# The first chunk of a windowed-attention and gated-FFN layer: layer norm tile by tile, its roots on GpSimd, and a first weight block for both halves of the array

## The chip, the cores and the metric

One NeuronCore of a Trainium2 chip runs one program. The metric is the device time of that program in microseconds, median of several runs. The engines are named as the profile names them: PE (TensorE), with PEld for its weight loads, DVE (VectorE), ACT (ScalarE), POOL (GpSimd) and SP (SyncE, which issues nearly all DMAs here). A "q" behind a name (SPq) is that engine's instruction queue. A column is one fp32 element of a partition.

## The reference

```python
def reference(A_x, A_wqkv, A_wo, B_x, B_w_gate, B_w_up, B_w_down):
    x = A_x                                   # (1, 2048, 512)
    xn = _layernorm(x, axis=-1)               # (x - mean) / sqrt(var + 1e-5)
    s = _A_ref(xn, A_wqkv, A_wo)              # 32 heads of 16, causal window of 256, softmax, @ wo
    g = _silu(_B_ref(xn, B_w_gate, B_w_up, B_w_down))   # (silu(xn@w_gate) * (xn@w_up)) @ w_down
    return x + s * g
```

The widths are D = 512 and F = 1792; everything is fp32. `B_x` is not used.

## The kernel before, in words

The 2048 tokens are worked on in four chunks of 512 (`c` = 0 to 3). For a chunk, `load_x(c)` fetches four tiles `xt` of 128 tokens by 512 features, takes mean and variance of each token (`stats`, L256 and L257), forms 1/sqrt(var + eps) in `rs`, and scales the tiles in place (`scale`). PE transposes the tiles into PSUM tiles `xp_0` to `xp_3`, one bank for each 128 features, 512 tokens wide. Each of these is split into two fp32r tiles that together hold the fp32 value: ACT copies it to the high part `xh` (a cast), and DVE subtracts that to get the low part `xl`. The raw weights `wr` are split in the same way, ACT making `wh` (L431) and POOL `wl` (L434). A product of two fp32 operands is three matmuls: high by high, and high by low both ways.

For chunk 0 this beginning has its own code. The fetches go out on two queues (SP and ACT). The roots of all four tiles are computed together on DVE once the last tile's statistics are in (`first_chain`: an initial guess by integer operations, then three Newton steps, L260 to L283), DVE scales the four tiles (L291), `x_turn` has PE transpose them (L351), and `x_split` makes `xh` (L344) and `xl` (L335), each over 512 tokens. For later chunks POOL takes the roots with a `pow` (L263 to L266) and ACT and POOL scale.

Until chunk 0 is there, PE multiplies a constant tile by itself or by an x tile (`warm_up`, L236), with results that nobody reads. It does so 20 times at the start, 13 times once the last x tile has landed, and 6 times behind the last transposes. One such fp32 matmul shows as two records in the trace.

The dense work is a fixed sequence of units of 1024 weight columns or less, each with two items: `Proj` (items `a_0`, `a_1`: queries and keys of a head group), `GateUp` (`g`, `u`), `Values` (`vp`), `Down` (`d`), `Wo` (`s`). The contraction is cut in two: rows 0 to 63 of the array (r = 0) and rows 64 to 127 (r = 1) run as two streams that work side by side, each with its own order (`pos[0]`, `pos[1]`). An item is first accumulated by r = 0; then DVE copies a column of the bank (`handover`, tile `ho`, L460), and r = 1 adds its share to the same bank. So r = 1 runs behind r = 0 by at least one item. Weight block j therefore holds the r = 0 rows of unit j and the r = 1 rows of unit j - 1 (`w_fetch`, `w_split`); raw blocks use a ring of two buffers, split ones a ring of three. Attention (scores `b` for the row maximum, a DMA of the maxima `ms` into the query tile `q`, scores `c`, `exp`, the product `pv`) is placed between the dense matmuls.

The order of all instructions is decided when the program is built. A planner keeps a virtual clock, estimated costs for V (DVE), S (ACT), G (POOL) and D (the DMA queue), and a list of ready jobs for each; `do(engine, ready, cost, fn, then, slack)` adds a job that is due at `ready + slack`, and the planner picks the job with the earliest due time. These costs decide the order only. On the chip each engine runs its instructions in that order and waits on semaphores.

Of the kernel before, what the change touches and what calls it, by code (L numbers as in the profile page):

```python
# [55 lines left out]
def tile_window_attention_swiglu_gate(  # L56
# [181 lines left out]
    def load_x(c):  # L238
# [5 lines left out]


        lnb = []
        if c == 0:
            lnb.extend(bank(rb_free, "ln"))
            ve, tm, r1 = (lnb[0][:, 4 * n : 4 * n + 4] for n in range(3))
            hv, t1 = (pers.tile([P, 4], F32, name=n) for n in ("hv", "t1"))  # L250

        def stats(i):
            st = sb(f"st{c}_{i}", [P, 6], F32, "st", 2)
            if c == 0 and i == 3:
                warm_up(xt[c, i][:, :P], 13)
            nc.vector.bn_stats(st, xt[c, i])  # L256
            nc.vector.bn_aggr(mv[:, i, :], st)  # L257

        def eps():
            nc.vector.tensor_scalar(ve, mv[:, :, 1], EPS, None, op0=ALU.add)  # L260

        def root():
            nc.gpsimd.tensor_scalar(ve, mv[:, :, 1], EPS, None, op0=ALU.add)  # L263
            nc.gpsimd.tensor_tensor(rs, ve, power[:, :4], op=ALU.pow)
            nc.gpsimd.tensor_tensor(tm, mv[:, :, 0], rs, op=ALU.mult)
            nc.gpsimd.tensor_scalar(tm, tm, -1.0, None, op0=ALU.mult)  # L266

        def roots(r=rs):

            i32 = mybir.dt.int32  # L270
            nc.vector.tensor_scalar(tm.bitcast(i32), ve.bitcast(i32), 1, None, op0=ALU.logical_shift_right)
            nc.vector.tensor_scalar(
                r.bitcast(i32), tm.bitcast(i32), -1, 0x5F3759DF, op0=ALU.mult, op1=ALU.add
            )

        def first_chain():
            eps()
            nc.vector.tensor_scalar(hv, ve, -0.5, None, op0=ALU.mult)
            roots(r1)
            for n in range(3):  # L280
                nc.vector.tensor_tensor(t1, r1, hv, op=ALU.mult)
                nc.vector.tensor_tensor(t1, r1, t1, op=ALU.mult)
                nc.vector.scalar_tensor_tensor(rs if n == 2 else r1, t1, 1.5, r1, op0=ALU.add, op1=ALU.mult)  # L283

        def scale(i):
            if c and i % 2 == 0:
                nc.scalar.activation(
                    xt[c, i], xt[c, i], AF.Identity, bias=tm[:, i : i + 1], scale=rs[:, i : i + 1]
                )
                return  # L290
            (nc.gpsimd if c else nc.vector).tensor_scalar(  # L291
                xt[c, i], xt[c, i], mv[:, i, 0:1], rs[:, i : i + 1], op0=ALU.subtract, op1=ALU.mult
            )
# [8 lines left out]
        def after_stats(t):  # L302
            left[0] -= 1
            if left[0] == 0 and c:
                do("G", t, 1.9, root, after_newton, sl)
            elif left[0] == 0:
                do("V", t, 2.5, first_chain, after_chain, -1.0)

        def after_chain(t):
            rb_free[lnb[1]] = t  # L310
            after_newton(t)

        def after_newton(t):
            for i in range(4):
                e = "SG"[i % 2] if c else "V"
                do(e, t, {"G": 2.1, "S": 0.62, "V": 0.55}[e], lambda i=i: scale(i), lambda t, i=i: scaled(t, i), sl + 0.3 * i)
# [6 lines left out]
        for i in range(4):  # L323
            dma(now[0], lambda i=i: fetch(i), lambda t, i=i: do("V", t, 0.8, lambda: stats(i), after_stats, sl),
                slack=0.1 * i, can=room(1) if c == 0 else room(5 - i + SPARE), e="S" if c == 0 and i % 2 else "D")

    xhigh = {}
    turned = []

    def x_split(c, k, pb, t, free):  # L330
        hi, lo = (xn[c % 2][s][:, k, :] for s in range(2))

        def low(t):
            xhigh[c, k] = t
            do("V", t, 0.61, lambda: nc.vector.tensor_tensor(lo, pb, f32(hi), op=ALU.subtract), done, -1.0)  # L335

        def done(t):
            free(t)
            xready[c, k] = t
            if k == KC - 1:  # L340
                for i in range(4):
                    give(xt.pop((c, i)))

        do("S", t, 0.52, lambda: nc.scalar.activation(hi, pb, AF.Copy), low, -2.0)  # L344


    def x_turn(i):
        if i == 0:
# [7 lines left out]
        if i == 3:  # L356
            warm_up(warm, 6)
            xstart[0] = False
            for k in range(KC):
                (pb, tag), p = turned[k]  # L360
                x_split(0, k, pb, now[0] + 0.2, lambda t, p=p, tag=tag: p.__setitem__(tag, t))

# [7 lines left out]

    class Unit:
# [3 lines left out]
        def wts(self, r):  # L379
            return wtile[self.n + r]  # L380
# [9 lines left out]

    def w_fetch(j):
        lo, up = weighted.get(j), weighted.get(j - 1)
# [5 lines left out]
        def go(r, u):  # L398
            if not box:
                box.append(sb(f"wr{j}", [P, 1024], F32, "wr", 2))  # L400
# [7 lines left out]
        for n, (r, u) in enumerate(parts):  # L408
            dma(now[0], lambda r=r, u=u: go(r, u), lambda t, n=n: then(t, n == len(parts) - 1),
                slack=1.0)  # L410

    def w_split(j):
# [4 lines left out]
        w = [weighted[i].width if i in weighted else 0 for i in (j, j - 1)]  # L417
# [15 lines left out]
        def low(pr, a, b):  # L433
            nc.gpsimd.tensor_tensor(lo[0][pr, a:b], raw[pr, a:b], f32(hi[0][pr, a:b]), op=ALU.subtract)  # L434

        def done(t):
            left[0] -= 1
            if left[0] == 0:
                wready[j] = t
                timer(t - 0.5, w_fetch, j + 2)  # L440

        for n, (pr, a, b) in enumerate(cuts):
            sl = (0.0 if j >= 3 else 0.2) + 0.3 * n
# [1027 lines left out]
```

## Time and profile before

| | |
|---|---|
| median of 3 runs | 871.76 us (870.12 to 876.5) |
| the profiled execution | 871.37 us; its span in the trace 869.7 us |
| granted TensorE clock | 0.999 |
| busy | PE 859.5 us, PEld 798.1, POOL 627.4, DVE 499.1, ACT 489.9 |
| DMA | 139.62 MB, mean 161 GB/s |
| first matmul of the first unit starts | 15.77 us |

A row of the timeline or of the chain of waits begins with its start and its length in us. A row of a group by line gives shortest, median and longest duration in ns. "x4" is a count of instructions.

### The profile page before, as it was taken

To read this page: it belongs to the slowest core of one execution; us is meant where nothing else is said; L and a number is where in the kernel's file an instruction comes from. 1 tells how busy PE (TensorE), PEld (TensorE's weight loads), DVE (VectorE), ACT (ScalarE), POOL (GpSimd) and SP (SyncE) were. 2 spreads that over 40 slices of the span, in tenths; PEclk is the share of its full clock that TensorE was granted. 3 is DMA by queue.
4 is the path that set the end of the run, shared out by engine and by line. 5 is a ranking of instruction groups with operands and counts; after the bars stand their busy time and mean duration, and the time that the engine had idled before them with its cause. 6 is when DMAs were issued, how large, how long until landed. Compare 5 with 4: busy or idle time off the path is not lost.

```text
span 869.7 us, 30126 instructions
## 1 busy us (share of the span) xinstructions
PE 859.5 (99%) x11966; PEld 798.1 (92%) x11966; DVE 499.1 (57%) x1650; ACT 489.9 (56%) x1046; POOL 627.4 (72%) x871
## 2 busy tenths in 40 slices
PE   9999999999999999999999999999999999999997
PEld 8899889899889998999999999899999999999897
DVE  5364466654765565766576666566555765554234
ACT  3345565555666466655566556655656665666431
POOL 5556587667777778767696798676768688869771
PEclk9999999999999999999999999999999999999999
DMA  5765846567676984766677987546666779644352
GB/s 148 187 167 121 221 115 168 126 162 167 148 198 180 251 201 105 152 156 133 155 184 194 214 200 181 129 145 151 158 150 173 174 187 209 162 130 112 108 126 74
DMA packets 69488, 139.62 MB, mean 161 GB/s; under 512 B 14546, under 2 KB 23250, under 8 KB 69348
## 3 DMA queue, kind: packets, MB, share of 16 engines
q1 hardware_dynamic: 69060, 137.18, 64.1%
q8 instruction: 94, 1.54, 0.8%
q10 hardware_dynamic: 288, 0.52, 0.2%
q14 instruction: 46, 0.38, 0.2%
HBM read 107.74 MB, written 29.62 MB: 158 GB/s over the span
## 4 chain that ended last, share of the span: by engine, by line
PE 93%; DMA 3%; DVE 1%; SPq 1%; POOL 0%; issue 0%; ACT 0%; ACTq 0%; DVEq 0%; POOLq 0%
PE u L463 18%; PE d L463 18%; PE g L463 17%; PE a L463 11%; PE pv L1148 8%; PE s L463 6%; PE c L1111 5%; PE vp L463 5%; PE b L960 4%; DMA q<-ms 1%; DMA r<-rd 1%; DMA xt<-x 1%; SPq L95 1%; DVE xt L291 0%; PE xp L481 0%
## 5 line engine op out<-in xcount | busy, mean ns | idle before, releaser
L434 POOL TENSOR_TENSOR wl<-wr,wh 128x512 fp32r<-128x512 f32 (+3 forms) x258 | 306.8, 1208 | 89.4 <-ACT wh L431 86.9
L968 DVE CUSTOM_DVE_ANT_0 jk<-b,maskb 128x384 bf16<-128x384 f32 (+2 forms) x512 | 271.5, 530 | 130.1 <-PE b L960 64.5
L1072 ACT ACTIVATE p<-c 128x384 f32<-128x384 f32 (+1 forms) x480 | 208.8, 489 | 127.1 <-PE c L1111 106.5
L463 PE MATMUL d<-wh,hh 64*128 64x256 f32 x1792 | 258.2, 278 | 0.0
L463 PEld LDWEIGHTS d<-wh,hh 64*128 64x128 f32 x1792 | 222.9, 185 | 1.0 <-issue 0.6
L463 PE MATMUL d<-wl,hh 64*128 64x256 f32 x896 | 201.3, 277 | 0.0
L431 ACT ACTIVATE wh<-wr 128x512 fp32r<-128x512 f32 (+3 forms) x258 | 142.2, 593 | 51.2 <-PE d L463 11.1
L463 PE MATMUL u<-xh,wh 64*128 64x512 f32 x448 | 167.3, 396 | 0.0
L463 PE MATMUL g<-xh,wh 64*128 64x512 f32 x448 | 167.2, 396 | 0.0
L463 PE MATMUL u<-xl,wh 64*128 64x512 f32 x448 | 166.9, 396 | 0.0
L463 PE MATMUL u<-xh,wl 64*128 64x512 f32 x448 | 166.9, 396 | 0.0
L463 PE MATMUL g<-xl,wh 64*128 64x512 f32 x448 | 166.5, 395 | 0.0
L463 PE MATMUL g<-xh,wl 64*128 64x512 f32 x448 | 164.8, 394 | 0.0
L1085 POOL TENSOR_SCALAR_AFFINE_SELECT p<-p 128x256 f32<-128x256 f32 x256 | 103.7, 410 | 77.1 <-ACT p L1072 75.6
L463 PEld LDWEIGHTS d<-wl,hh 64*128 64x128 f32 x896 | 144.4, 185 | 0.3
L960 PE MATMUL b<-k,q 48*128 48x384 f32 (+1 forms) x512 | 119.2, 333 | 0.0
L1111 PE MATMUL c<-q,k 49*128 49x384 f32 (+1 forms) x704 | 115.5, 302 | 2.3 <-DMA q<-ms 1.2
L1089 POOL TENSOR_SCALAR_AFFINE_SELECT p<-p 128x256 f32<-128x256 f32 x224 | 91.6, 410 | 13.2 <-ACT p L1072 13.1
L463 PE MATMUL a<-xh,wh 64*128 64x512 f32 x256 | 97.2, 394 | 0.0
L463 PE MATMUL a<-xh,wl 64*128 64x512 f32 x256 | 96.4, 392 | 0.0
L616 POOL TENSOR_TENSOR hh<-h,hh 128x512 fp32r<-128x512 f32 x56 | 72.5, 1295 | 33.0 <-ACT hh L612 32.7
L463 PE MATMUL a<-xl,wh 64*128 64x512 f32 x256 | 96.2, 393 | 0.0
(109 smaller groups left out, 2096.6 us busy)
## 6 DMA issues: line engine op xcount, KB each, us to landing
wr<-wgu SPq DMA_DIRECT2D x112, 256.0 KB
k<-qkd SPq DMA_DIRECT2D x48, 192.0 KB
wr<-wqk SPq DMA_DIRECT2D x32, 256.0 KB
qkd<-qkh SPq DMA_DIRECT2D x32, 256.0 KB
qkd<-qkl SPq DMA_DIRECT2D x32, 256.0 KB
q<-qkd SPq DMA_DIRECT2D x64, 128.0 KB
wr<-wdn SPq DMA_DIRECT2D x32, 256.0 KB
od<-ev SPq DMA_DIRECT2D x32, 256.0 KB
```

What stands on the lines that cost most here:

```text
L95: eng.dma_start(dst, src)
L431: nc.scalar.activation(hi[0][pr, a:b], raw[pr, a:b], AF.Copy)
L434: nc.gpsimd.tensor_tensor(lo[0][pr, a:b], raw[pr, a:b], f32(hi[0][pr, a:b]), op=ALU.subtract)
L463: return nc.tensor.matmul(pb, a, b, start=first, stop=last, skip_group_check=True)
L616: nc.gpsimd.tensor_tensor(hl[:, 1, :], self.h, f32(hl[:, 0, :]), op=ALU.subtract)
L960: nc.tensor.matmul(pb[:, :w], qs[u % 3][r : r + 48, p, qb * P : (qb + 1) * P], ks[u % 3][r : r + 48, p, lo : lo + w], start=True, stop=True,)
L968: nc.vector.tensor_tensor_reduce(junk[:, :n], pb[:, :n], maskb[:, 3 * P - n :], 1.0, -3.0e38, ALU.add, ALU.max, m[:, col : col + 1],)
L1072: nc.scalar.activation(t[:, h, :], pc[:, a:b], AF.Exp, scale=DH ** -0.5)
L1085: nc.gpsimd.affine_select(s, s, [[0, 2], [1, P]], ALU.is_ge, 0.0, base=0, channel_multiplier=-1)
L1089: nc.gpsimd.affine_select(s, s, [[0, 2], [-1, P]], ALU.is_gt, 0.0, base=0, channel_multiplier=1)
L1111: nc.tensor.matmul(pc[:, at0 : at0 + w], ks[u % 3][r : r + 49, p, k0 : k0 + P], qs[u % 3][r : r + 49, p, qb * P : qb * P + w], start=(i == ...
L1148: nc.tensor.matmul(pbs[r][0][32 * j : 32 * j + 32, q0:q1], vt[half(r), (4 * c + kb) % VT, VW * (4 * g + j) : VW * (4 * g + j) + 32], t[hal ...
```

## The change

- **Roots.** For chunk 0 DVE adds eps to the variance of a tile right behind its statistics. POOL then takes a `pow` over one column for each tile, and for the first two tiles that came also the product -mean * rs. The Newton chain on DVE is gone.
- **Scaling.** The first two tiles that came are scaled by ACT (`Identity` with scale and bias), the other two by DVE. `x_turn` takes the tiles in that order.
- **Splitting.** `x_split` works on parts of 256 tokens: part 0 is due once tiles 0 and 1 are transposed, part 1 after tiles 2 and 3. In the first item (`a_0`) each matmul goes over 256 tokens, in the order wh by xh, wl by xh, wh by xl.
- **Weights.** Block 0 now holds both row halves of unit 0 (`block(n, r)`), block 1 only the r = 0 half of unit 1, block 2 the usual pair; block 2's raw tile gets a buffer of its own and is fetched from 8.5 us of the planner's clock on. The first item may start once the first half of block 0's high part is made. POOL's first low part waits behind a one-column copy (`spare`) that reads the last scaled x tile.
- **Constant matmuls.** 7 at the start, then, from 4.1 us of the planner's clock on, one at a time while no tile is there to be turned: 19 ahead of the first transposes, 2 and 3 between them, none behind them.

The diff, cut to its core:

```diff
@@ load_x
-        if c == 0:
-            lnb.extend(bank(rb_free, "ln"))
-            ve, tm, r1 = (lnb[0][:, 4 * n : 4 * n + 4] for n in range(3))
...
         def stats(i):
+            came.append(i)
-            if c == 0 and i == 3:
-                warm_up(xt[c, i][:, :P], 13)
             nc.vector.bn_stats(st, xt[c, i])
             nc.vector.bn_aggr(mv[:, i, :], st)
+            if c == 0:
+                nc.vector.tensor_scalar(ve[:, i : i + 1], mv[:, i, 1:2], EPS, None, op0=ALU.add)
...
+        def root(a, b):
+            if c:
+                nc.gpsimd.tensor_scalar(ve, mv[:, :, 1], EPS, None, op0=ALU.add)
+            nc.gpsimd.tensor_tensor(rs[:, a:b], ve[:, a:b], power[:, a:b], op=ALU.pow)
+            if c == 0 and side(a) == "S":
+                nc.gpsimd.tensor_scalar(
+                    tm[:, a:b], mv[:, a, 0:1], rs[:, a:b], -1.0, op0=ALU.mult, op1=ALU.mult
+                )
...
+        def side(i):
+            return "SG"[i % 2] if c else "SSVV"[came.index(i)]
@@ x_split
+        n = slice(256 * part, 256 * part + 256)
+        hi, lo = (xn[0][s][:, k, n] for s in range(2))
...
@@ x_turn
-        if i == 3:
-            warm_up(warm, 6)
-            xstart[0] = False
+        seen.add(i)
+        part = i // 2
+        if {2 * part, 2 * part + 1} <= seen:
             for k in range(KC):
                 (pb, tag), p = turned[k]
-                x_split(0, k, pb, now[0] + 0.2, ...)
+                x_split(k, part, pb, now[0] + 0.2, ...)
@@ weights
+    def block(n, r):
+        return n + r if n else 0
+    def units_of(j):
+        return weighted.get(j), weighted.get(j - 1 if j else 0) if j != 1 else None
...
+                if j == 2:
+                    box.append(pers.tile([P, 1024], F32, name="wr2", tag=f"hr{NHID - 1}", bufs=1))
...
         def low(pr, a, b):
+            if j == 0 and a == 0:
+                nc.gpsimd.tensor_copy(spare, xt[0, list(normed)[-1][1]][:, :1])
             nc.gpsimd.tensor_tensor(lo[0][pr, a:b], raw[pr, a:b], f32(hi[0][pr, a:b]), op=ALU.subtract)
@@ Stationary.mms
+            if self.c == 0 and self.n == 0 and i == 0:
+                for a, b in ((0, 0), (1, 0), (0, 1)):
+                    for part in range(2):
+                        for k in range(KC):
...
@@ start and main loop
-    warm_up(warm, 20)
+    warm_up(warm, 7)
...
+    timer(8.5, w_fetch, 2)
...
+        if xstart[0] and now[0] >= 4.1:
+            warm_up(warm, 1)
+            advance(0.4267 if now[0] < 6.9 else 0.2234)
```

What the change does to the order is seen at three places. The numbers behind a name (`xp_0_175`) are buffer numbers. The first place is PE from the last transposes that stood before the constant matmuls to the second item. Before:

```order
L351 MATMUL xp_3_209<-ident,xt_3_139 128x128
L236 MATMUL warm<-warm 128x128 x6
L463 MATMUL a_0_244<-xh_79,wh_194 128x512
L463 MATMUL a_0_244<-xh_79,wl_195 128x512
L463 MATMUL a_0_244<-xh_79,wh_194 128x512
L463 MATMUL a_0_244<-xh_79,wl_195 128x512
L463 MATMUL a_0_244<-xh_79,wh_194 128x512
L463 MATMUL a_0_244<-xh_79,wl_195 128x512
L463 MATMUL a_0_244<-xh_79,wh_194 128x512
L463 MATMUL a_0_244<-xh_79,wl_195 128x512
L463 MATMUL a_0_244<-xl_80,wh_194 128x512 x4
L463 MATMUL a_1_265<-xh_79,wh_194 128x512
```

and now:

```order
L341 MATMUL xp_3_178<-ident,xt_3_124 128x128
L236 MATMUL warm<-warm 128x128 x3
L341 MATMUL xp_0_175<-ident,xt_2_126 128x128
L341 MATMUL xp_1_176<-ident,xt_2_126 128x128
L341 MATMUL xp_2_177<-ident,xt_2_126 128x128
L341 MATMUL xp_3_178<-ident,xt_2_126 128x128
L470 MATMUL a_0_218<-xh_79,wh_199 128x256 x8
L470 MATMUL a_0_218<-xh_79,wl_200 128x256 x8
L470 MATMUL a_0_218<-xl_80,wh_199 128x256 x8
L470 MATMUL a_1_262<-xh_79,wh_199 128x512
L470 MATMUL a_1_262<-xl_80,wh_199 128x512
L470 MATMUL a_1_262<-xh_79,wl_200 128x512
```

The tiles are turned in the order 1, 0, 3, 2 now, the constant matmuls stand ahead of the last tile's transposes, and the first item's 12 matmuls became 24 of half the width with all eight wh-by-xh ones in front. The second place is ACT from the scaled tiles to block 0's second half, with the engine that each row waits for:

```order
L271 ACTIVATE xt_1_120<-xt_1_120,tm_92,rs_91 128x512 [waits DMAHW0_49,DVE_49,Pool_49]
L271 ACTIVATE xt_0_122<-xt_0_122,tm_92,rs_91 128x512 [waits DMAHW1_49,DVE_49,Pool_49]
L429 ACTIVATE wh_199<-wr_132 128x512 [waits DMAHW7_49,DMAHW0_49]
L333 ACTIVATE xh_79<-xp_0_175 128x256 [waits PE_49]
L333 ACTIVATE xh_79<-xp_1_176 128x256 [waits PE_49]
L333 ACTIVATE xh_79<-xp_2_177 128x256 [waits PE_49]
L333 ACTIVATE xh_79<-xp_3_178 128x256 [waits PE_49]
L333 ACTIVATE xh_79<-xp_0_175 128x256 [waits DVE_49]
L333 ACTIVATE xh_79<-xp_1_176 128x256 [waits DVE_49]
L333 ACTIVATE xh_79<-xp_2_177 128x256 [waits DVE_49]
L333 ACTIVATE xh_79<-xp_3_178 128x256 [waits DVE_49]
L429 ACTIVATE wh_199<-wr_132 128x512
```

Before, ACT stood at four `wh` rows (blocks 0 and 1), then four `xh` rows of 512, each waiting for PE alone. Now the first `wh` row waits for both halves of block 0 to land and stands ahead of all `xh` rows, and the `xh` rows of part 1 wait for DVE: in the program each waits for the low part of part 0 in the same bank. The rows of part 0 wait for transposes of the tile 3 (`xp_0`, `xp_1`) and of the tile 2 (`xp_2`, `xp_3`), which lie in part 1. The third place is SP's queue behind the x tiles; the difference reads:

```order
 L95 DMA k_75<-one 2x512 x3
-L95 DMA wr_147<-wqk 64x1024
+L95 DMA wr_132<-wqk 64x1024 x2
 L95 DMA k_76<-one 2x512 x2
-L95 DMA wr_173<-wgu 64x1024
-L95 DMA wr_173<-wqk 64x1024
+L95 DMA wr_163<-wgu 64x1024
 L95 DMA k_76<-one 2x512
 L95 DMA k_77<-one 2x512 x3
```

Unit 0's second half (256 KB) moved ahead of two small copies of a constant row into `k`, and takes the place in the queue where the first of these stood; unit 1's half moved up by one place.

More of the change, by code (lines that the diff above doesn't have):

```diff
@@ L257, in stats @@
             nc.vector.bn_aggr(mv[:, i, :], st)
[L259 to L274, printed above, removed]
```

123 lines of the change are left out of this document (68 added, 55 removed).

## The prediction

> **What bounds the kernel now.** I read the busy shares first, then the chain of waits as a whole, then the chain and the timeline of the first 25 us, where the change lies.
>
> ```profile
> PE   859.5 (99%) x11966; PEld 798.1 (92%) x11966; DVE 499.1 (57%) x1650; ACT 489.9 (56%) x1046; POOL 627.4 (72%) x871
> PE 93%; DMA 3%; DVE 1%; SPq 1%; POOL 0%; issue 0%; ACT 0%; ACTq 0%; DVEq 0%; POOLq 0%
> ```
>
> PE is never short of work for long, and the chain that ends last is PE for 93% of the span. What can be won is therefore time in which PE does work that nobody needs, and the beginning is such a time. The chain of waits there:
>
> ```profile
> 1.22 5.20 DMA xt<-x
> ...
> 10.44 0.17 DVE rs L283
> 10.64 3.16 DVE xt L291 x4
> 13.84 0.66 PE xp L351 x4
> 14.50 1.34 PE warm L236 x12
> 15.84 5.86 PE a L463 x33
> ```
>
> The x tiles are awaited until 6.42, then DVE alone sets the pace for over 7 us (statistics, Newton chain to 10.61, four scalings to 13.80), then come transposes and constant matmuls, and useful matmuls start near 15.8. The third view is PE's timeline:
>
> ```profile
> 1.10 7.52 PE L236 MATMUL warm<-warm 128*128 128x128 f32 x40 [1.10 <-DVE warm L231]
> 8.46 3.07 PE L236 MATMUL warm<-xt,warm 128*128 128x128 f32 x26
> 11.61 1.50 PE L351 MATMUL xp<-ident,xt 128*128 128x128 f32 x12
> ...
> 14.33 1.50 PE L236 MATMUL warm<-warm 128*128 128x128 f32 x12
> ...
> 17.74 1.10 PE L463 MATMUL a<-xl,wh 64*128 64x512 f32 x4
> 18.68 0.39 PE L463 MATMUL a<-xh,wh 64*128 64x512 f32 x1
> ```
>
> I take the start of the second item (`a_1`, 18.68) as the mark. From there on both streams have work; before and after it the same matmuls follow, so the mark's shift is the kernel's shift unless something later gives it back.
>
> **The statistics** gain an instruction for each tile.
>
> ```profile
> 4.68 0.69 DVE L256 BATCH_NORM_STATS2 st<-xt 128x6 f32<-128x512 f32 x1 [3.63 <-DMA xt<-x]
> 5.41 0.18 DVE L257 BATCH_NORM_AGGREGATE mv<-st 128x2 f32<-128x6 f32 x1
> 5.51 0.66 DVE L256 BATCH_NORM_STATS2 st<-xt 128x6 f32<-128x512 f32 x1
> ...
> 7.97 0.18 DVE L257 BATCH_NORM_AGGREGATE mv<-st 128x2 f32<-128x6 f32 x1
> 8.19 0.17 DVE L260 TENSOR_SCALAR ln<-mv 128x4 f32<-128x4 f32 x1
> ```
>
> A tile takes 0.83 (5.51 - 4.68). The eps addition that depends on the aggregate starts 0.22 behind it (8.19 - 7.97), so a tile takes about 1.05 and the tiles start at 4.68, 5.73, 6.78 and 7.83. The last one's eps ends at 7.83 + 0.73 + 0.22 + 0.17 = 8.95, against 8.36 now: 0.6 lost.
>
> **Roots and scaling.** Durations by line, for the later chunks where such rows exist, and one row of POOL's timeline:
>
> ```profile
> L264 POOL TENSOR_TENSOR rs<-ve,power x3: 1050/1051/1052, 121.0 to 504.6; 128x4 f32<-128x4 f32 x3
> L265 POOL TENSOR_TENSOR tm<-mv,rs x3: 202/203/203, 122.1 to 505.7; 128x4 f32<-128x4 f32 x3
> L287 ACT ACTIVATE xt<-xt,tm,rs x6: 798/809/817, 122.7 to 508.6; 128x512 f32<-128x512 f32 x6
> L291 DVE TENSOR_SCALAR xt<-xt,mv,rs x4: 533/680/1490, 10.6 to 12.3; 128x512 f32<-128x512 f32 x4
> ...
> 11.95 2.96 POOL L434 TENSOR_TENSOR wl<-wr,wh 128x512 fp32r<-128x512 f32 x2 [0.78 <-ACT wh L431]
> ```
>
> No row shows a `pow` of one column. Its bounds are 0.20 (an ordinary product of four columns) and 1.05 (the `pow` of four). The difference, 0.85 for four columns, makes 0.21 for one, so I take 0.2 + 0.21 and a gap, 0.45, nearer to the lower row because the work falls with the columns. Tiles one and two also need a product of about 0.25 on POOL; they are scaled by ACT at 0.81 each, done by 7.5 and 8.6, under the statistics of the later tiles and so free. The path is the last tile: eps at 8.95, root at 9.46, DVE's scaling 0.53, end 10.03. The third tile's scaling fits ahead of it (8.95 to 9.48). The shortest L291 row is the right one: the fourth, from 12.3 to 13.8, ran beside POOL's subtraction of weights (11.95 to 14.91), and that is now held back by `spare`. Against 13.80 this is 3.8 us earlier. If `pow` costs 1.05, four of them and two products stand in a row on POOL (from 5.85: 1.05 + 0.25 + 1.05 + 0.25 + 1.05 + 1.05 with gaps of 0.1), the last ends near 11.1 instead of 9.46 and the gain falls by 1.6 to 2.2; at 0.20 it grows by 0.25.
>
> **From the last scaled tile to the mark.** This took 18.68 - 13.80 = 4.88 before. Now ACT first needs block 0, which is twice as large. Queue and ACT rows:
>
> ```profile
> 3.63 0.53 SPq L95 DMA_DIRECT2D wr<-wqk  x1
> 4.68 1.00 SPq L95 DMA_DIRECT2D k<-one  x2
> ...
> 6.99 0.60 SPq L95 DMA_DIRECT2D wr<-wqk  x1
> ...
> 7.97 1.15 ACT L431 ACTIVATE wh<-wr 64x512 fp32r<-64x512 f32 x2 [4.76 <-DMA wr<-wqk]
> ...
> 11.24 1.16 ACT L431 ACTIVATE wh<-wr 128x512 fp32r<-128x512 f32 x2 [2.12 <-DMA wr<-wqk]
> ```
>
> 256 KB took 4.34 us from its issue to the waiting ACT row (3.63 to 7.97) and 4.25 (6.99 to 11.24). The second half of block 0 is issued at 4.68, where the first `k` copy stood: landing 9.0, and the first `wh` half lasts to 9.6. At the 5.2 of the x tile in the chain it would land at 9.9, the upper bound; no row is shorter than 4.25. The two `k` copies behind it shift by 0.5 and are first read with the first queries, long after: nothing. Unit 1's half goes out near 7.0 as before.
>
> PE turns tile 3 at 9.5, does its three constant matmuls (six records at 3.07 / 26 = 0.118) to 10.7 and turns the last tile until 11.1. ACT has meanwhile made two highs of part 0. The other rows:
>
> ```profile
> 14.21 2.06 ACT L344 ACTIVATE xh<-xp 128x512 fp32r<-128x512 f32 x4 [1.81 <-PE xp L351]
> L499 ACT ACTIVATE xh<-xp x24: 378/384/419, 140.0 to 542.4; 128x256 fp32r<-128x256 f32 x24
> L496 DVE TENSOR_TENSOR xl<-xp,xh x24: 409/416/425, 140.4 to 542.9; 128x256 fp32r<-128x256 f32 x24
> 833.52 15.55 PE d L463 x265
> ```
>
> ACT took a bank 0.37 after its transpose began (14.21 - 13.84), so `xp_2`'s high of part 0 starts near 11.3. Four rows of 512 took 2.06, so a row of 0.60 costs 0.52 in a series and one of 0.38 about 0.30. The two remaining highs of part 0 last to 11.9, the four of part 1 to 13.1; DVE's lows of part 0 (from 11.05, every 0.35) are each ready in time. Matmuls of 256 columns cost 15.55 / 265 = 0.059 with two streams, 0.117 in one, half of the 0.234 of 512 (18.68 - 17.74, by four): cutting an item in 24 costs nothing. Behind the last high stand 17 of them, 2.0 us; POOL's first low part (10.4 to 11.7) and DVE's lows (to 13.9) are ahead of their readers. The mark falls at 13.15 + 2.0 = 15.15: 5.1 us behind the scaled tile, 0.2 more than before.
>
> **Sum.** 18.68 - 15.15 = 3.5 us; 871.37 - 3.5 = 867.9. The profiled execution lies 0.4 below the median of the runs shown, so their median would come to 868.3; I say 868.0. As the program is PE after the mark, no gain beyond this can come from there.
>
> **What speaks against it.** In the order, part 1's highs wait for part 0's lows of the same bank, although they touch other columns. The Trainium skill, "PSUM — Partial Sum Buffer", section "PSUM bank collisions raise a hardware error", asks for just this: two engines must not touch one bank and 32-partition quadrant at once, two readers included. No run here shows a collision. With these waits the sum is 867.9, as above; without them all eight highs would run in one series from 9.95, with part 1 from 11.2 to 12.5, and it would be 867.3.
>
> **What is late next.** Everything behind the mark comes 3.5 us earlier, so weights and attention must follow.
>
> ```profile
> 23.39 2.54 POOL L434 TENSOR_TENSOR wl<-wr,wh 128x512 fp32r<-128x512 f32 x2 [3.99 <-ACT wh L431]
> ...
> 31.67 0.39 PE L463 MATMUL g<-xh,wl 64*128 64x512 f32 x1
> ```
>
> Block 3 was split by 25.93 and its low part first read at 31.67: 5.7 us to spare, 2.2 after the shift, even if its split does not move at all: its fetch waits for POOL's second low part of block 0, which by the sum above ends near 15 us (ACT's second `wh` half follows the highs until 13.7, POOL's subtraction takes 1.3). That holds, so I cost it at nothing; if the split slipped by 3 us, PE would wait 0.8.
>
> **Rivals.** (1) *The clock falls.* From 11.1 to 13.1 PE has eight short matmuls and no constant ones. The first 40 constant records ran at 188 ns, later ones at 118: PE starts slow and speeds up. The start loses 40 x 0.07 = 2.8 us by it; if it came again the time would be 870.7. Against it: from 11.61 to 14.33 only 16 transposes ran, and the 12 records behind them took 125 ns each. "TensorE: Matmul & The Clock Gate" of the Trainium skill, Part 1, lets the clock halve after an idle window of about 3.4 us. By that rule the stretch is too short, and the trace agrees as far as its 2.7 us go.
>
> (2) *Roots or landing late*, the upper bounds above: a `pow` near 1.05 or block 0 at 9.9 instead of 9.0. Then 1.0 to 2.2 go and the time is near 869.5. This is also the case in which the change hardly does what it says.
>
> (3) *A wait downstream takes the gain.* Rows of the waits, the chain and the timeline:
>
> ```profile
> PE c L1111 <- DMA q<-ms: 1.2, 2, 0.6
> 54.09 5.34 DMA q<-ms
> ...
> 45.09 1.10 SPq L95 DMA_DIRECT2D wr<-wv  x1
> ...
> 51.06 1.15 ACT L431 ACTIVATE wh<-wr 128x512 fp32r<-128x512 f32 x2
> ...
> 53.80 0.27 ACT L1009 ACTIVATE ms<-mt 16x128 fp32r<-16x128 f32 x1
> ```
>
> PE's scores `c` already waited 0.6 at 59.4 for the maxima. If this chain doesn't move with PE, PE waits 3.5 longer: 871.4, no change. For it: POOL's and SP's work on weights is bound by landings, not by PE. Against it: the maxima come from PE's own scores, which move with the mark.
>
> (4) *Slower.* ACT's `ms` row stands behind block 8's highs (51.06), now with a tanh between, then directly. After the change ACT needs that raw block at 51.06 - 3.5 = 47.6. Its issue is now at 45.09, so at 4.3 us it lands at 49.4. If that did not move at all, 1.8 of the gain would go; from a landing at 51.1 on the kernel is slower than before, and each us more costs one: 872.5 at 52.2. For it: the fetch waits for POOL and for queries and keys ahead of it on SP. Against it: all of these start from PE's results or from weights with room, so it would have to come 1.7 later than now while its causes come earlier.
>
> **How the numbers follow.** Forecast 0.64 (866.8 to 868.8, from `pow` at 0.20 and a landing within 0.5); rival 2 0.14; rival 1 0.10; rival 3 0.08; rival 4 0.04. The range reaches from 866.4 (the forecast's lower end and a scatter of 0.4, the gap between profiled run and median) to 871.0; outside lie rivals 3 and 4 and half of that scatter, under 2 in 10. About 1% (8.7 us) is what a measurement can tell from no change: faster by more would need the mark at 10.0, when the last tile is only just scaled; slower by more a loss of 12 us, four times any price above. So 0.02, 0.96, 0.02.
>
> **What would show it.** Right: no Newton rows; one-column `pow` rows near 0.4; the last scaling ending near 10.0; the first `wh` row at 9.0; `xh` rows to 13.1; `a_1` at 15.2; no new PE wait before 60 us. Wrong: `pow` near 1 us, `wh` waiting for `wr` past 9.5, matmuls of 256 columns spaced 0.2 behind 13 us, or a PE wait for `q<-ms` of several us.

## The result

| | before | after |
|---|---|---|
| median of 17 runs each | 872.51 us (869.12 to 878.51) | 867.19 us (865.61 to 870.57) |
| ratio, 95% interval | | 0.994 (0.9924 to 0.9957) |
| the profiled execution; its span | 871.37; 869.7 us | 866.04; 864.2 us |
| `a_1` starts (the mark) | 18.68 us | 15.14 us (forecast 15.15) |

The kernel became 5.3 us faster by the medians (3.8 to 6.6 by the interval), 3.5 of it at the start, as forecast. That is less than 1%, the middle one of the prediction's three cases. The page of the changed kernel, its busy shares and the chain of waits by engine:

```profile
PE 857.4 (99%) x11960; PEld 799.3 (92%) x11960; DVE 495.0 (57%) x1643; ACT 492.0 (57%) x1052; POOL 630.0 (73%) x878
PE 97%; DMA 1%; DVE 1%; issue 0%; POOL 0%; ACT 0%; SPq 0%; DVEq 0%; ACTq 0%
```

PE's part of the chain rose from 93% to 97%. The start of the chain of waits after the change (start, length, what):

```profile
1.11 7.37 PE warm L236 x38
8.48 0.44 PE xp L341 x4
...
10.23 0.67 PE warm L236 x6
10.90 0.44 PE xp L341 x4
11.34 6.87 PE a L470 x48
```

DVE's Newton chain and scalings are gone from it; useful matmuls start at 11.3 instead of 15.8. The timeline shows the steps (start, length, engine, line, operation, output and inputs, count, idle time before it and what ended that):

```profile
5.86 0.58 POOL L257 TENSOR_TENSOR rs<-ve,power 128x1 f32<-128x1 f32 x1 [1.67 <-DVE ve L252]
8.81 0.78 POOL L257 TENSOR_TENSOR rs<-ve,power 128x1 f32<-128x1 f32 x1 [0.46 <-DVE ve L252]
8.59 0.63 ACT L429 ACTIVATE wh<-wr 128x512 fp32r<-128x512 f32 x1
9.62 0.55 DVE L275 TENSOR_SCALAR xt<-xt,mv,rs 128x512 f32<-128x512 f32 x1 [0.44 <-POOL rs L257]
10.74 0.60 PE L341 MATMUL xp<-ident,xt 128*128 128x128 f32 x4
11.27 1.76 ACT L333 ACTIVATE xh<-xp 128x256 fp32r<-128x256 f32 x6 [0.67 <-PE xp L341]
15.14 0.39 PE L470 MATMUL a<-xh,wh 64*128 64x512 f32 x1
```

The last tile is scaled by 10.17 (9.62 + 0.55) and turned by 11.34, ACT's highs end at 13.03 (11.27 + 1.76), and the mark follows 2.1 behind them.

The rest of the gain lies behind the mark. Rows of the chain that stand at the same place of the program, before:

```profile
166.97 1.86 PE pv L1148 x56
264.12 2.38 PE pv L1148 x93
694.46 2.38 PE pv L1148 x93
```

and after:

```profile
162.38 1.88 PE pv L1160 x56
257.58 2.38 PE pv L1160 x93
688.89 2.38 PE pv L1160 x93
```

The distance is 3.54 at the mark, then 4.59, then 6.54, then 5.57: it grows twice and something is given back. The waits of PE say where it grows (total, number, longest). Before, behind the mark, beside the 1.2 for `q<-ms` that the prediction shows:

```profile
PE c L1111 <- DVE m L968: 1.1, 1, 1.1
PE mt L994 <- DVE ho L460: 0.9, 1, 0.9
```

and after, as the only wait behind the mark but one of 0.2 that both have (at 213 us in the kernel before):

```profile
PE b L972 <- DMA k<-qkd: 0.6, 1, 0.6
```

So 3.2 us of waits became 0.6. By their places they account for 1.1 us of the first step and 1.5 of the 1.95 of the second; the 1.0 that is given back later stands in no wait of this view. Whether the drop in waits belongs to the change was the first question. The second came from the spread of the changed kernel. Its 17 executions, time in us and mean granted clock:

```
0.998 or 0.999: 865.61 865.72 865.85 865.87 865.92 866.04 866.31 866.51 867.19 867.23 868.77
0.995 to 0.997: 867.42 867.94 868.39 869.07 870.16 870.57
```

### The profile page after: what moved, and what is told of

Same layout as the page of the kernel before. It is cut to its first block, busy times and chain, and to the rows that moved or that the text cites. A ratio compares the mean times of both kernels' runs of the same rounds, so it can differ in the third digit from the quotient of the medians.

```text
span 864.2 us, 30118 instructions
## 1 busy us (share of the span) xinstructions
PE 857.4 (99%) x11960; PEld 799.3 (92%) x11960; DVE 495.0 (57%) x1643; ACT 492.0 (57%) x1052; POOL 630.0 (73%) x878
## 4 chain that ended last, share of the span: by engine, by line
PE 97%; DMA 1%; DVE 1%; issue 0%; POOL 0%; ACT 0%; SPq 0%; DVEq 0%; ACTq 0%
PE u L470 18%; PE g L470 18%; PE d L470 18%; PE a L470 12%; PE pv L1160 8%; PE s L470 6%; PE c L1123 5%; PE vp L470 5%; PE b L972 4%; PE warm L236 1%; DMA wr<-wqk 1%; DMA k<-qkd 0%; PE xp L488 0%; DVE jk L980 0%; POOL wl L434 0%
## 5 line engine op out<-in xcount | busy, mean ns | idle before, releaser
L434 POOL TENSOR_TENSOR wl<-wr,wh 128x512 fp32r<-128x512 f32 (+2 forms) x258 | 306.6, 1208 | 83.0 <-ACT wh L429 76.0
L429 ACT ACTIVATE wh<-wr 128x512 fp32r<-128x512 f32 (+2 forms) x258 | 142.0, 594 | 44.1 <-PE d L470 11.1
L972 PE MATMUL b<-k,q 48*128 48x384 f32 (+1 forms) x512 | 117.1, 333 | 0.6 <-DMA k<-qkd 0.6
L470 PE MATMUL a<-xh,wh 64*128 64x512 f32 (+1 forms) x264 | 97.0, 389 | 0.0
L470 PE MATMUL a<-xh,wl 64*128 64x512 f32 (+1 forms) x264 | 95.6, 385 | 0.0
L470 PE MATMUL a<-xl,wh 64*128 64x512 f32 (+1 forms) x264 | 95.6, 385 | 0.0
```

What stands on the lines that cost most here:

```text
L429: nc.scalar.activation(hi[0][pr, a:b], raw[pr, a:b], AF.Copy)
L470: return nc.tensor.matmul(pb, a, b, start=first, stop=last, skip_group_check=True)
L972: nc.tensor.matmul(pb[:, :w], qs[u % 3][r : r + 48, p, qb * P : (qb + 1) * P], ks[u % 3][r : r + 48, p, lo : lo + w], start=True, stop=True,)
```

## The experiments

All orders not named in an edit are those of the kernel that it starts from. The mark is again the first `a_1` row, and the time stands against the kernel before, on the same chip. Where no ratio is given, the time is that of a single execution, and the changed kernel's own executions spread over 5 us.

**1 and 2. Both kernels again, unchanged.**

> The kernel before, unchanged, profiled a second time. Its first trace shows five PE waits behind the mark: 0.6 near 59 us, 1.1 near 104, 0.9 near 238, 0.6 near 248 (and 0.2 near 119 in both kernels), 3.2 us without the last. Theory 'start only' (the change is worth the 3.5 us of the mark, the rest of the difference is which landings PE happens to wait for in an execution): the mark is at 18.6 to 18.8 again, but the waits behind it differ by 1 us or more in their sum, or stand at other places. Theory 'order' (the program as it was planned anew behind the mark is worth the other 1.8 us in every execution): the same waits at the same places, 3.2 us in all within 0.5.

> The changed kernel, unchanged, profiled a second time. Its first trace shows the mark at 15.14 and behind it PE waits of 0.6 (scores b for a copy of keys, near 39 us) and 0.2. 'Start only': mark 15.1 to 15.3, and PE waits behind it whose sum differs from 0.8 by 0.5 us or more, at other places too. 'Order': again 0.6 and 0.2 and nothing else.

Times 873.05 and 867.63. The waits behind the mark in the second profile of the kernel before:

```profile
PE c L1111 <- DMA q<-ms: 2.9, 4, 1.0
PE mt L994 <- DVE ho L460: 0.5, 1, 0.5
PE g L463 <- issue: 0.4, 1, 0.4
```

and in that of the changed kernel:

```profile
PE c L1123 <- DMA q<-ms: 0.9, 2, 0.5
PE s L470 <- issue: 0.9, 1, 0.9
```

The marks repeat within 0.3 (18.90 and 15.09). The sums of the waits do not: 3.8 after 3.2, and 1.8 after 0.6. In the changed kernel the places change too. In the kernel before, the four places of the first profile (near 59, 104, 238 and 248 us) wait again, by 0.5 to 1.1, and two more for `q<-ms` are added (0.5 and 1.0). Two profiles each can't yet say whether the kernel before waits more by its order.

**3. The new order with the old start.**

```diff
@@ x_turn of the changed kernel
         if len(seen) == 4:
             xstart[0] = False
+            warm_up(warm, 19)
```

> The changed kernel with 19 more constant matmuls on PE behind the last transposes; every instruction behind them stays in the order of the changed kernel, on all engines. 19 x 2 records x 0.118 = 4.5 us, and since the splits are then ready when PE comes, the first item runs in 24 x 0.117 = 2.8 us: the mark comes to 11.34 + 4.5 + 2.8 = 18.6, where it was before. 'Start only': the whole gain is gone, the ratio to the kernel before is 1.000 (0.998 to 1.002). 'Order': the order behind the mark keeps its 1.8 us, 0.998 (0.996 to 0.9995). A third theory, 'lead': the weights and copies now have as much time ahead of PE as before, so that the wait for the copy of keys (0.6) goes as well and PE waits for nothing: 0.997.

```profile
18.58 0.39 PE L471 MATMUL a<-xh,wh 64*128 64x512 f32 x1
PE c L1124 <- DMA q<-ms: 1.3, 3, 0.6
PE b L973 <- DMA k<-qkd: 0.2, 1, 0.2
```

The mark (first row, timeline) is back at 18.58, and so is nearly the whole time: 871.6, ratio 0.9991 (0.9979 to 1.0003). What the order behind the mark is worth by itself is 0.8 us, from 1.8 down to less than nothing. The ratio lies in the ranges of both "start only" and "order", so this run alone does not decide between them. "Lead" falls: the waits (next two rows) did not go.

**4. Roots at once.**

```diff
@@ load_x, chunk 0
-                do("G", t, ..., lambda: root(i, i + 1), lambda t: scale_of(t, i), -1.0)
+                left[0] -= 1
+                if left[0] == 0:
+                    do("G", t, 1.6, roots4, lambda t: [scale_of(t, j) for j in came], -1.0)
...
```

> The changed kernel with the roots of the first chunk in one pow over four columns behind the last statistics (two products behind it), the rest kept: eps by tile, two tiles scaled by ACT and two by DVE, parts of 256. (23 constant matmuls ahead of the transposes, and ACT's block 1 behind the splits, so that neither stands in the way.) Theory 'tile by tile is where the gain is': statistics end 8.7, pow 1.05 to 9.9, products to 10.4, DVE scales until 11.0 and ACT until 11.9; the last tile is 1.7 later than now, the mark comes to 15.9 (if the splits overlap better) to 16.8. Rival, 'taking the roots off the Newton chain is the gain': the last root is only 0.3 later than now (9.9 against 9.6), the mark is at 15.4 or earlier.

Time 871.8 (before 872.77), mark 18.82. The timeline:

```profile
9.21 1.05 POOL L267 TENSOR_TENSOR rs<-ve,power 128x4 f32<-128x4 f32 x1 [5.00 <-DVE ve L252]
10.36 1.07 POOL L269 TENSOR_SCALAR tm<-mv,rs 128x1 f32<-128x1 f32 x2
10.92 1.52 ACT L278 ACTIVATE xt<-xt,tm,rs 128x512 f32<-128x512 f32 x2 [0.77 <-POOL tm L269]
14.57 1.68 PE L480 MATMUL a<-xh,wh 64*128 64x256 f32 x8 [1.25 <-ACT xh L342]
```

ACT had scaled the last tile at 12.44 (10.92 + 1.52), and the first item started at 14.57. The change had moved that start from 15.77 to 11.27; 3.3 of these 4.5 us are lost again. Tile by tile is where most of the gain is, not the removal of the Newton chain alone. The mark came 2 us later still than the upper end of what was expected. The stretches of the program (length, busy time of PE and the other engines, then granted clock, DMA share and GB/s) explain half of that:

```profile
12.90:16.80 3.90, 2.65 (x19) 2.13 (x18) 2.74 (x8) 3.77 (x12) 3.17 (x3) 1.00 0.19 26
16.90:23.60 6.70, 6.70 (x43) 6.60 (x43) 0.15 (x1) 0.46 (x1) 3.98 (x4) 0.50 0.54 150
```

The granted clock was 0.50 for 6.7 us, which costs half of them, 3.4 us. Only the first 2 of them lie ahead of the mark, so the fall delayed the mark by 1; the other 1 us is a last tile scaled 0.5 later than expected and a first item paced by ACT. The fall was rival 1 of the prediction, and the next four runs are about it.

**5. The same with PE kept busy:** 34 instead of 23 constant matmuls ahead of the transposes.

> The run with the roots at once, with 11 more constant matmuls ahead of the transposes (34 instead of 23), so that PE is busy until 12.0 instead of 9.1. In that run the granted clock fell to 0.50 from about 17 to 23.4, and its mark stood at 18.82. Theory 'the pause did that': the clock stays at 1.00, and what is left is the roots' own price: highs from 13.4 on, the first useful matmul near 14.9 and the mark at 14.9 + 24 x 0.117 = 17.7, 2.5 later than in the changed kernel; time 869.7. Rival: the clock falls in any case, and the mark is at 19 or later.

```profile
9.50:12.90 3.40, 3.40 (x32) 3.19 (x31) 1.00 (x2) 1.94 (x3) 2.21 (x5) 1.00 0.48 131
12.90:16.30 3.40, 2.15 (x15) 1.63 (x14) 2.74 (x8) 3.33 (x11) 2.66 (x3) 1.00 0.15 46
16.40:23.10 6.70, 6.70 (x41) 6.60 (x41) 0.15 (x1) 0.90 (x2) 4.41 (x4) 0.50 0.64 155
```

The clock fell all the same, the mark was 19.20 and the time 875.15 (before 871.91). PE was full until 12.9, so the early pause was not the cause. What came just ahead of the fall is a stretch with a wait of 1.25 us and the start of the first item.

**6. No hold on POOL.**

```diff
@@ w_split
-            if j == 0 and a == 0:
-                nc.gpsimd.tensor_copy(spare, xt[0, list(normed)[-1][1]][:, :1])
...
-            do("G", t, 0.17 + 0.0021 * (b - a), lambda: low(pr, a, b), lambda t: done(t, a), sl, lambda: len(normed) >= 4)
+            do("G", t, 0.17 + 0.0021 * (b - a), lambda: low(pr, a, b), lambda t: done(t, a), sl)
```

> The changed kernel without the one-column copy that holds POOL's first subtraction of weights until the last x tile is scaled; nothing else changes its place. POOL then subtracts from 9.6 on, beside DVE's scaling of the last tile. Theory 'they get in each other's way' (the row of 1.49 us in the first kernel, against 0.53): the last scaling takes 1.3 to 1.5 instead of 0.55, the last tile is 0.75 to 0.95 later, and so is the mark: 15.9 to 16.1. Rival: the two don't disturb each other, the long row had another cause, and the mark stays at 15.1.

```profile
10.15 1.49 DVE L275 TENSOR_SCALAR xt<-xt,mv,rs 128x512 f32<-128x512 f32 x1 [0.44 <-POOL rs L257]
13.90:20.60 6.70, 6.70 (x36) 6.60 (x37) 1.12 (x4) 2.76 (x6) 5.91 (x5) 0.50 0.32 81
```

DVE's scaling beside POOL's subtraction (10.09 to 11.36) took 1.49 again instead of 0.55. So `spare` buys what the prediction took for it. The first item started 1.1 later (12.35). Not all of this is the scaling: the x tiles landed 0.5 later in this execution (first statistics at 5.14 instead of 4.61). Experiment 3, whose statistics began as late (5.17), turned its last tile from 10.96, this run from 11.79, so 0.8 us belong to the scaling, as expected. The mark came at 17.95 and not at 16, since the clock fell here too (second row). Time 869.59.

**7. None between the transposes.**

```diff
@@ main loop
         if xstart[0] and now[0] >= 4.1:
-            warm_up(warm, 1)
+            if not seen:
+                warm_up(warm, 1)
```

> The changed kernel without the five constant matmuls between the transposes; the 19 ahead of them stay, and the order of all else. The last tile is turned when it is scaled (10.2) and not 0.55 later. If the granted clock stays at 1.00: the mark comes 0.5 earlier, 14.6, and the time 0.5 with it, ratio to the kernel before 0.9935. Theory 'the clock falls when PE has only transposes and pauses': from 8.5 to 10.8 it has nothing else (2.3 us, against 5.4 us in the run with the roots at once, whose granted clock fell to 0.50 for some 6.5 us); then matmuls of 256 columns stand 0.21 apart for some us and 3 us are lost: 870.

```profile
10.67 0.63 PE L341 MATMUL xp<-ident,xt 128*128 128x128 f32 x4 [0.42 <-ACT xh L333]
12.00:15.40 3.40, 3.40 (x24) 2.98 (x24) 1.86 (x7) 3.40 (x9) 1.82 (x2) 1.00 0.35 84
15.50:18.80 3.30, 3.30 (x24) 3.30 (x25) 0.00 (x0) 0.10 (x1) 3.30 (x4) 0.50 0.60 160
18.90:22.00 3.10, 3.10 (x31) 2.62 (x31) 0.85 (x2) 0.60 (x1) 0.92 (x1) 1.00 0.01 3
```

The mark stayed at 15.10: the last tile's transposes wait for ACT's highs of the same banks (first row), not for the constants, so these five cost next to nothing (the marks of the two unchanged profiles are 15.14 and 15.09). But they are worth a lot: median 870.16, ratio 0.9985 (0.9969 to 1.0001), and all ten executions had a mean clock of 0.994 to 0.997. The time is the 870 of the second theory, but not by its path: the first item ran at full clock, and the fall came behind the mark. The clock was 0.50 from about 15.4 to 18.8, although PE counts as busy for the whole 3.4 us ahead of it.

**8. No constants at all.**

> The changed kernel without any constant matmul; the order of all else is kept. PE's first work is the first transpose, near 8.3. Theory 'the constants buy the clock': the first item's 24 matmuls take 0.21 each instead of 0.117, the mark comes to 11.3 + 5.0 = 16.3 or a little later, PE stays slow for some us behind it, and the time is 3 to 4 us longer than the changed kernel's, 870 to 871. Rival 'they buy nothing': the mark comes 0.5 earlier as in the run without the five, and the time is 866.7.

```profile
14.41 1.91 PE L470 MATMUL a<-xl,wh 64*128 64x256 f32 x8
16.12 0.62 PE L470 MATMUL a<-xh,wh 64*128 64x512 f32 x1
14.40:21.10 6.70, 6.70 (x43) 6.60 (x43) 0.15 (x1) 1.34 (x3) 5.61 (x5) 0.50 0.29 78
```

The mark, 16.12, is near the 16.3 that "the constants buy the clock" expected, but only a third of the mechanism was there. The first eight matmuls were paced by ACT's highs as in the changed kernel, the next eight ran 0.12 apart, and only the last eight, from 14.41 on (first row), stood 0.21 apart. The clock fell at 14.3 and not ahead of the item. The time, 868.59 (before 871.91), is 1.4 better than expected. At that clock a matmul of 512 columns takes 0.62 (second row) instead of 0.39.

**9. Constants inside the first item.**

```diff
@@ Stationary.mms, first item
-                                return mm(pb[:, n], w[a][half(r), i, k, :], xs[b][half(r), k, n], first, last)
+                                mm(pb[:, n], w[a][half(r), i, k, :], xs[b][half(r), k, n], first, last)
+                                if r == a == b == 0 and k % 2 == 0:
+                                    warm_up(warm, 1)
```

> The changed kernel with four constant matmuls (8 records of 0.118) set between the first eight matmuls of the first item, behind the first and third of each four, where PE waits for ACT's splits anyway; all other order is kept. Of the 17 executions of the changed kernel 11 had a mean clock of 0.998 or 0.999 (865.6 to 868.8, median 866.0), six 0.995 to 0.997 (867.4 to 870.6). Theory 'the clock is granted by how full the array was in a window of 3.4 us, and the half-filled first item is at the edge': with the fill no execution falls below 0.998, the mark is at 15.2, the median at 866.1 and the highest under 868.8; ratio to the kernel before 0.9925. Rival 'the clock's falls have another cause': a third of the executions are again at 0.997 or below, median 867.2, ratio 0.994.

```profile
11.54 0.49 PE L236 MATMUL warm<-warm 128*128 128x128 f32 x2
11.95 0.50 PE L470 MATMUL a<-xh,wh 64*128 64x256 f32 x2
```

Missed on both counts. A constant matmul (128 rows) between two matmuls of 64 rows takes 0.41 until the next one starts (11.54 to 11.95), not 0.24, so the mark moved to 16.60; and three of twelve executions still had a mean clock of 0.994 to 0.997, too few to tell this from the six of 17. Median 869.86, ratio 0.9966 (0.9949 to 0.9983).

**10. Weight blocks as before:** block 0 with the r = 0 rows alone.

```diff
@@ weights
     def block(n, r):
-        return n + r if n else 0
+        return n + r
     def units_of(j):
-        return weighted.get(j), weighted.get(j - 1 if j else 0) if j != 1 else None
+        return weighted.get(j), weighted.get(j - 1)
...
```

> The changed kernel with its weight blocks as before: block 0 holds unit 0's r = 0 rows alone, block 1 unit 1's r = 0 rows and unit 0's r = 1 rows, no own buffer for block 2. ACT's two halves of 64 rows (1.15 us) end near 9.8, before the first high could start (9.94): the mark stays at 15.1 to 15.3. Behind it r = 1 finds its rows later: eight matmuls of a_1 run alone instead of three, 5 x 0.234 = 1.2 us. Theory 'r = 1 trails for the rest of the program': 0.6 to 1.2 us longer than the changed kernel. Rival 'r = 1 catches up': no loss, 866 to 867.2. Apart from that: if the waits that both profiles of the kernel before show near 104 and 238 to 249 us (0.7 to 1.1 and 1.2 to 1.5 us) stand here again, they come from the blocks' order; if not, they do not.

```profile
14.98 0.39 PE L466 MATMUL a<-xh,wh 64*128 64x512 f32 x1
PE c L1119 <- DMA q<-ms: 1.0, 1, 1.0
```

The mark is even 0.16 earlier, so the start owes nothing to the new blocks. r = 1 began 0.36 later than in the changed kernel (15.91 against 15.55), where 1.2 was expected. The ratio is 0.0015 above the changed kernel's, about 1.3 us, but the intervals overlap, so neither theory is settled. The waits of the kernel before (near 104 and 238 to 249 us) do not stand in this one profile, so the old blocks at least do not make them in every execution; others do, of 1.0 for `q<-ms` and 0.6 for `k<-qkd`. Median 869.04, ratio 0.9955 (0.9937 to 0.9973), four of twelve executions at 0.994 or 0.995.

**11. The kernel before without its six constants** behind the last transposes.

```diff
@@ x_turn of the kernel before
         if i == 3:
-            warm_up(warm, 6)
             xstart[0] = False
```

> The kernel before without its six constant matmuls behind the last transposes (12 records, 14.33 to 15.67), the one part of the change that costs nothing to write; all other order is kept. Theory 'the six stand on the path': the first item starts near 14.6 instead of 15.77 and is paced by ACT's highs (0.52 each) and DVE's lows, the mark comes to 17.3 to 17.5 instead of 18.68, 1.2 to 1.4 us less, ratio to the kernel before 0.9985, within its interval. Rival 'they hold the clock up': PE then has 16 transposes from 11.6 on and right behind them the first item, on half of the array; if the granted clock falls as in the runs without constants, 1.7 us for each window of 3.4 us are lost, mean clocks of 0.995 to 0.997 stand in most executions, and the ratio is 1.000 to 1.003.

```profile
18.07 0.40 PE L462 MATMUL a<-xh,wh 64*128 64x512 f32 x1
245.14 0.51 PE L1110 MATMUL c<-q,k 49*128 49x256 f32 x4 [0.93 <-DVE m L967]
```

Mark 18.07: 0.6 earlier, half of what was expected, because the last tile was scaled 0.25 later in this execution and then ACT and DVE set the pace. Median 872.12, ratio 1.0007 (0.9987 to 1.0027); three of twelve executions were at 0.994 or 0.995. The one line alone wins nothing that can be measured. Behind its mark this program has exactly the order of the kernel before, yet apart from the 0.2 of both kernels this profile shows one wait, of 0.9 (second row), and none near 59, 104 or 238 us. So most of the 3.2 and 3.8 us of the two earlier profiles is not fixed by that order. The 0.9 is different: it stands at the same matmul of the scores `c`, with 128 matmuls of this line ahead of it in each trace, that waited in both profiles of the kernel before:

```profile
248.22 0.50 PE L1111 MATMUL c<-q,k 49*128 49x256 f32 x4 [0.57 <-DMA q<-ms]
248.36 0.51 PE L1111 MATMUL c<-q,k 49*128 49x256 f32 x4 [0.66 <-DMA q<-ms]
```

All three profiles with the old order wait there, 0.6 to 0.9. None of the seven profiles whose order behind the mark is the changed kernel's (its two, and experiments 3 and 6 to 9) has a PE wait between 225 and 262 us.

**12. A version meant to beat both.**

```diff
@@ x_split, x_turn: a bank holds one part of two feature groups
+        pb = pb[:, 256 * (k % 2) : 256 * (k % 2) + 256]
...
-                (pb, tag), p = turned[k]
+                (pb, tag), p = turned[2 * part + k // 2]
...
+        if len(seen) == 3:
+            warm_up(warm, 2)
@@ Stationary.mms, first item
-                for a, b in ((0, 0), (1, 0), (0, 1)):
-                    for part in range(2):
+                for part in range(2):
+                    for a, b in ((0, 0), (1, 0), (0, 1)) if part else ((0, 0), (0, 1), (1, 0)):
```

> A version meant to beat both: each PSUM bank holds one part of 256 tokens of two feature groups instead of both parts of one, so that part 1's transposes and highs no longer wait for part 0's; the first item goes through part 0 and then part 1 (highs by highs, then for part 0 wh by xl ahead of wl by xh); of the five constant matmuls between the transposes only two stay, behind the third tile. The last tile is turned until 10.7, ACT's highs end at 11.9 instead of 13.0, PE starts the first item at 10.75 and is not short of input any more: mark at 10.75 + 24 x 0.117 = 13.6, at most 13.9, against 15.14. Theory 'the bank waits and the order set the mark': 1.3 to 1.5 us less than the changed kernel's undisturbed 866.0, 864.7, ratio 0.991. Rival 'the clock falls, since PE has mostly transposes from 8.5 to 10.7': mean clocks of 0.995 to 0.997, 2 to 3 us more in most executions, 867, ratio 0.994.

```profile
9.54 2.51 ACT L335 ACTIVATE xh<-xp 128x256 fp32r<-128x256 f32 x8
10.94 0.74 PE L474 MATMUL a<-xh,wh 64*128 64x256 f32 x4
13.79 0.39 PE L474 MATMUL a<-xh,wh 64*128 64x512 f32 x1
```

ACT's eight highs run in one series until 12.05, PE goes through the first item without a gap, and the mark is at 13.79, within the 13.6 to 13.9 expected. Median 864.92, ratio 0.9914 (0.9894 to 0.9935), five executions, all with a mean clock of 0.998 or 0.999. It is faster than the kernel before for certain; against the changed kernel its interval overlaps by 0.001, and the 1.35 us of the mark are what is shown. The banks, the first item's order and the constants changed together here, so how the 1.35 divide among them is not shown, and five executions are too few to say that the clock's falls are gone.

## Why the prediction was right, point by point

- **The mark: 15.15 forecast, 15.14 found.** The path was the forecast one; the agreement to 0.01 is luck, as some of its terms were off both ways. Statistics: eps of the last tile ends at 8.72 (forecast 8.95). The hold on POOL and the 0.53 of DVE's scaling: right, and experiment 6 shows the 1.49 that it avoids.
- **Roots: mis-sized.** One column takes 0.55 to 0.58, and 0.78 beside DVE, where the working took 0.41. "The work falls with the columns" was the weak step: 1.05 for four and 0.56 for one mean a fixed part near 0.4. The last root took 0.37 more than in the working; as its eps was 0.23 earlier, it ended only 0.13 late (9.59 against 9.46).
- **Landing: mis-sized the other way.** ACT split block 0 at 8.59, not from 9.0, so at most 4.0 from the issue of its second half near 4.6, under the bound of 4.25. The two errors touch different inputs, and neither reached the mark.
- **Transposes.** The last tile was turned until 11.34, not 11.1, and by ACT's highs rather than by the constants (experiment 7). The highs end at 13.03 (forecast 13.1), and 2.1 us later (2.0) stands the mark. The waits between the parts were there, and the sum with them was the right one; experiment 12 takes them away by other banks, together with two other edits. Whether a collision would happen without them no run shows.
- **The failed step: "no gain beyond this can come from there".** PE does wait behind the mark, 0.9 to 3.8 us in three profiles with the order of before and 0.6 and 1.8 in two of the changed kernel. The wait view had shown them. Most of them vary from one execution to the next, so the difference between two profiles (5.5 us of span) held 2 us that the change didn't bring for certain. By the timed runs 0.8 us (-0.3 to 1.8) stay when the old mark is restored. The wait at the one score near 248 us, 0.6 to 0.9 in every profile with the old order and absent with the new one, would be of that size; no run tests it by an edit. Together with the start's 3.5 the 0.8 is inside the interval of the gain.
- **A sign that failed: "no new PE wait before 60 us".** PE waits 0.6 near 38 us for a copy of keys (`k<-qkd`, shown with the result). A wait for that copy, of 0.2 to 0.6, stands in seven of the eleven profiles of the changed kernel and its variants, and in none of the three of the kernel before and its variant. The working counted the copies of the constant row into `k` at nothing, and did not look at this one.
- **How near the time came is partly luck.** The median, 867.19, is 0.8 below the forecast's 868.0. The eleven executions with a clock of 0.998 or 0.999 have 866.0, 2 below it and under the forecast's 866.8; the falls of the clock in the other six took 1.2 of that back. Of the 6.5 us by which those eleven beat the kernel before, 3.5 are the start and 0.8 the order by experiment 3; no experiment accounts for the other 2.
- **Rivals 3 and 4** did not come: no wait for `q<-ms` in the first profile after, 0.9 in the second, and no PE wait for weights in either.
- **Rival 1, the clock, was taken too lightly.** Its price was about right: 3.41 us at 0.50 cost 1.7, two such stretches 3.4. The reason against it was not: that 16 transposes alone had not brought the clock down. What follows them differs. Before, 12 constant records came next, and then a first item on 64 of the 128 rows whose input was ready; now such an item follows at once, fed at ACT's pace. Experiment 11 fits this: without the 12 records three of twelve executions of the old kernel had 0.994 or 0.995. With them 7 of 69 had 0.996 or 0.997 in the rounds of the experiments, so falls are rarer there but not absent. Six of the 17 executions of the changed kernel had a mean clock below 0.998; their median is 868.7 against 866.0 for the other eleven. The fall itself is shown in the profiles of experiments 4 to 8, and inferred from the mean clock for these six, whose profiles were not kept.
- **The Trainium skill on this**, "TensorE: Matmul & The Clock Gate", Part 1: the gate looks at a free-running window of 3413 ns and falls to half after an idle one. The lengths agree (0.50 for some 3.4 us in experiment 7, 6.8 in 4, 5, 6 and 8). A free-running window would explain why the same program falls in some executions only, which no run here shows. "Idle" does not agree: the stretch ahead of the fall in experiment 7 has PE busy for 3.40 of 3.40 us in the profile (which models where matmuls end), with matmuls on 64 rows, the first of them spaced by ACT. By these rows something short of idle is enough; how little use of the array that is stays open, since experiment 9 put more on the array and three of twelve executions still fell.

## What to carry to other kernels

Find the one event from which everything behind it is full, sum up to it, and treat waits behind it as a spread of their own: two profiles of one kernel differed there by up to 1.2 us, and two executions of the changed kernel in their whole time by up to 5. Look in several profiles whether a wait stands at the same instruction before calling it chance or order. Constant matmuls that look useless can be free and still hold up the clock, so look at the granted clock for some 10 us behind every stretch in which PE is fed slowly or on half its rows. Where two engines take turns on a PSUM bank, try a cut by which each bank holds what is ready at the same time; here such a cut, with two other edits, moved the mark by 1.35 us.

## What the runs showed of the hardware that was not expected

- The granted clock halves for 3.4 us although PE counts as busy for the whole 3.4 us ahead of it and from its first matmul on never paused for more than 0.52 us (experiment 7). In experiments 4 to 6 and 8, where PE had waited 0.7 us or more, it halves for 6.8 us.
- A `pow` of one column on POOL takes 0.56, of four 1.05; beside a DVE scaling the first takes 0.78, and a product of one column 0.53 instead of 0.26 (experiment 4).
- A 128-row fp32 constant between two 64-row matmuls costs 0.41 until the next start instead of the 0.24 that its two records take in a row (experiment 9).
